# A transformer stack ordered by a planner: a longer modelled delay from ScalarE to TensorE, and five scheduler constants

## Chip, core and metric

The kernel runs on one core of one Trainium2 chip. The metric is the time of one execution on the device in microseconds, as the median over several runs. Five engines work beside each other, each through its own list in order: TensorE (PE in the profile), VectorE (DVE), ScalarE (ACT), GpSimd (POOL) and the DMA queue of SyncE (SP).

## What is computed

Two layers of attention and two of a feed-forward network over 2048 tokens of width 448, with the same weights in both rounds. There are 16 heads of width 28, and the hidden width is 1792.

```python
def _A_ref(x, wqkv, wo):            # S = 2048, D = 448, H = 16, Dh = 28
    qkv = (x @ wqkv).reshape(B, S, 3, H, Dh).transpose(2, 0, 3, 1, 4)
    q, k, v = qkv[0], qkv[1], qkv[2]
    p = softmax(einsum("bhqd,bhkd->bhqk", q, k) * Dh ** -0.5)
    o = einsum("bhqk,bhkd->bhqd", p, v)
    return o.transpose(0, 2, 1, 3).reshape(B, S, D) @ wo
def _B_ref(x, w1, b1, w2, b2):
    h = relu(einsum("bsd,df->bsf", x, w1) + b1)
    return einsum("bsf,fd->bsd", h * h, w2) + b2

x = x + _A_ref(layernorm(x), A_wqkv, A_wo)
x = x + _B_ref(layernorm(x), B_w1, B_b1, B_w2, B_b2)
x = x + _A_ref(layernorm(x), A_wqkv, A_wo)
x = x + _B_ref(layernorm(x), B_w1, B_b1, B_w2, B_b2)
```

## The kernel before

**Units and groups.** Queries are cut into blocks of 256 (the last two of layer 1 into blocks of 128), heads into four sets g of four. A pass is one block, one g and a range of keys. A unit is 512 columns of scores of one head: two tiles of 128 keys by 256 queries, or four by 128. There are 2048 units, 1024 for each layer. `s_stream` puts three units at a time into a tile `sc` of three PSUM banks, of which there are two, so TensorE can be two groups ahead of ScalarE at most. `e_stream` takes the exponential of a group on ScalarE (L835), into one of 11 buffers `pt` (NPT). `p_stream` multiplies with V (L984, "PV"), up to two blocks of keys at a time, accumulating into `oT`.

**The takeover.** `apart` may give the third unit of a group to VectorE, which computes the exponential by a polynomial: `a_unit` and `a_rest`, five instructions (L891, L905, L911, L917, L924). ScalarE's instruction on that group is then 1024 columns wide, not 1536. The unit taken is the next in order, or, when fewer than LAG units remain of the pass, one of the next pass. VectorE has two working sets for this (`R_v`; `v_i`/`v_e`, and a stretch of the K tile not in use). `apart` declines when no set is free, when the load of VectorE over the last 14 us of the plan is above BUSY (0.95), or, where `behind` is true, above LOW (0.8). `behind` compares the chain work done with a straight line given by LINES: from unit a to unit b, n chains. A chain's work is counted as 0.8 for each addition after the output projection, 1 for each full activation tile, 2.8 for each addition after the second matrix, and in layer 0 another 6 for the next layer's Q, K and V; so 14.2 (1.6 + 7 + 5.6) or 20.2 in all for a block.

**The chains.** When all heads of a block are ready, `chain` runs the output projection, layer norm, the first matrix with relu and square, the second matrix, and in layer 0 the Q, K and V of layer 1. VectorE empties most of its PSUM tiles (L1162, L1115, L576, L604 and others). Such work goes to TensorE between the score groups.

**The planner.** The whole order of instructions is decided before launch by a list scheduler, `Planner`. Streams offer their next operation; `earliest` works out when it could start from the modelled ends of what it depends on, plus the delay LAT of the producing engine, and when buffers come free. Those same delays are added when a buffer is released. `run` takes the candidate with the earliest start, priorities deciding ties. Work for TensorE other than scores ("filler") is admitted only if it ends before the score group's due time plus `slack()`:

```python
due = next((c[3][2].ready for c in cands if c[1] == 0), None)
ok = [c for c in cands if c[2] != "PE" or c[1] == 0 or c[0] + c[3][2].dur <= due + self.slack()]
```

`slack()` is SLACK less 512/1200 for each unit that is missing in the group before. The planner's durations are n/1200 + 0.05 us for an exponential over n columns, 0.22 for a group of scores, 0.04 + 0.22 for each block of keys of PV, and 0.1 for changing the shape in which the array is used. Scores are followed by the exponential after 0.25 us.

**Repeats and heating.** Where TensorE's load would be low, scores are issued again, up to three times more (`o.more`, and `again` at L801: as many repeats of 0.22 us as fit before the end of the exponential before, less 0.30 us). `heat` (L1205) also issues idle matmuls (L1220).

**PV and its waits.** `p_stream` prefers key blocks that are ready. It waits for the next exponential rather than for an unfinished unit of VectorE, as long as the oldest group concerned is less than NPT - KEEP groups behind ScalarE (L963).

Of the kernel before, what the change touches and what calls it, by code (L numbers as in the profile page):

```python
# [35 lines left out]
DCLK = 0.2  # L36
OWN = 2
HALF = 320
LINES = ((280, 1312, 7.6), (1440, 2040, 6.6))
MARGIN = 2.0  # L40
LOW = 0.8
TURNS = 1
# [7 lines left out]
GATE = [None, None, ('Q', 0, 0, 0), ('Q', 0, 0, 0), ('s', 8), ('s', 8), ('s', 8), ('s', 8)]  # L50
EARLY = 2
AHEAD = (range(0, 4), range(0, 4), range(0, 4))
SLACK = 0.5
WINDOW = 2.8
C_PRIO = 1.5
V_PRIO = 7.0
# [7 lines left out]
V_WAIT = 5.5  # L64
NEAR = 9
FAR = 15
KEEP = 3
LAG = 5
LEAD = 20
LAST = 690  # L70
BUSY = 0.95
# [46 lines left out]
        self.need, self.got, self.more = need, [], 0.0  # L118


LAT = {"PE": 0.25, "ACT": 0.22, "DVE": 0.10, "POOL": 0.15, "DMA": 2.0, "-": 0.0}


class Planner:
# [3 lines left out]
    def __init__(self):  # L128
# [5 lines left out]
        self.turns = lambda: False  # L134
        self.slack = lambda: SLACK

# [9 lines left out]
    def earliest(self, o):  # L146
        t = 0.0
        for d in o.deps:
            if not isinstance(d, Op):
                d = self.tok.get(d)  # L150
            if d is None or d.end is None:
                return None, None
            same = d.eng[0] == o.eng[0] and len(o.eng) == 1
            t = max(t, d.end + d.lat + ((0.03 if same else 0.10) if d.eng[0] == "DVE" else
                                (0.0 if same and d.eng[0] != "DMA" else LAT[d.eng[0]])))
        acq = o.acq() if callable(o.acq) else o.acq
# [15 lines left out]
    def run(self):  # L172
        while self.streams:
# [9 lines left out]
            if due is None:  # L183
                due = next((c[0] + c[3][2].dur + LAT["ACT"] for c in cands if c[1] == 1), None)
            if due is not None:
# [20 lines left out]
            for a in o.rel:  # L206
                a.got.append(o.end + o.lat + LAT[e])
                if len(a.got) == a.need:
# [9 lines left out]
def kernel(  # L218
# [214 lines left out]
    def slack():  # L433

        n = gbuf[-2]["n"] if len(gbuf) > 1 else 3
        return SLACK - (3 - n) * 512 / 1200

# [251 lines left out]
    def behind(i):  # L689

        l = 0 if i < LINES[0][1] else 1
        a, b, n = LINES[l]
        return done[l] < (min(i, b) - a) / (b - a) * n * per[l] - MARGIN
# [10 lines left out]
    def apart(i, now, us, soon=SOON):  # L704
# [6 lines left out]
        j = i  # L711
        if i + LAG > ends_at[units[i][0]]:
            j = ends_at[units[i][0]] + 1
# [9 lines left out]
        if held[0] + 1 > min(sum(r.n for r in pd_free(units[k])) for k in (i, j)):  # L723
            return None
        if any(pl.tok.get(d) is None or pl.tok[d].end + LAT["DVE"] > now for d in needs(units[j])):
            return None
# [13 lines left out]
    def needs(unit):  # L740
        pi, kb, r, hh = unit
        l, qb, g, *_ = passes[pi]
        t0, nt = blocks[l][qb]
        return [("K", l, g, kb + i) for i in range(r)] + [("Q", l, g, t0 + i) for i in range(nt)]

    def s_stream():
        while at[0] < len(units):
# [5 lines left out]
            def fn(e, gi=gi, us=us, js=js):  # L753
# [45 lines left out]
                if short > 0 and gi > 0:  # L799
                    last = ("e" in gbuf[gi - 1] and gbuf[gi - 1]["e"].end) or pl.clock["ACT"] + 1.35  # L800
                    again = max(0, min(MORE, int(min(o.room, last - LAT["PE"] - 0.05 - o.end) / 0.22)))  # L801
                o.more = 0.22 * again
# [131 lines left out]
    def p_stream():  # L934


        for pi, (l, qb, g, kbs, first, last) in enumerate(passes):
# [18 lines left out]
            while todo:  # L956
                now = [kb for kb in todo if done(kb)][:some]
                if len(now) < min(some, len(todo)):
                    kb = next(kb for kb in todo if not done(kb))
                    if ("u", pi, kb) not in pl.tok or any(k < 3 and ("e", gi) not in pl.tok for gi, k, _ in where[pi, kb]):  # L960
                        yield from got(kb)
                        continue
                    if (e_now[1] - min(gi for gi, _, _ in where[pi, kb]) < NPT - KEEP and e_now[1] < len(gbuf) - 1  # L963
                            and len(todo) > len(now) + 1):
# [306 lines left out]
```

## Time and profile before

| | |
|---|---|
| median of 5 runs | 882.87 us (882.46 to 883.41) |
| the profiled execution | 882.87 us, span 881.0 us |
| ScalarE busy | 866.9 us (98%), 707 instructions |
| TensorE busy | 825.7 us (94%), 12796 matmuls |
| VectorE busy | 794.7 us (90%), 1568 instructions |
| GpSimd busy | 39.3 us (4%) |
| exponentials on ScalarE | 683: 528 of 1536 columns, 155 of 1024 |
| units on VectorE | 154 (87 in the first working set, 67 in the second) |
| granted TensorE clock | 1.000 of full speed |

The span is the time from the first to the last instruction of one profiled execution; 1.87 us of its time lie outside. Busy time is the union of an engine's records. A row "A <- B: us, times, longest" of the waits says how long A's engine sat idle until B released it. Records of ScalarE overlap, so its busy time hides short gaps; the starts of neighbouring records do not.

### The profile page before, as it was taken

The page shows a single profiled execution, that of the slowest core. Times are in us where ns is not written, and L with a number is a line of the kernel's source. Part 1 is how long each engine was busy: PE and PEld are TensorE (multiplying, and loading weights), DVE is VectorE, ACT ScalarE, POOL GpSimd, SP SyncE. Part 2 cuts the span into 40 slices and gives each one's busy share as a digit, 9 for nine tenths or more (in the row PEclk, how much of TensorE's full clock was granted, in tenths as well). Part 3 has the DMA queues.
Part 4 walks back from the last instruction along what each step waited for, and adds up shares of the span by engine and source line. Part 5 has one row for each costly group of instructions (what it writes and reads, how often), then busy time and mean ns, then how long its engine had stood idle before and what let it go on. Part 6 is the DMA issues. An engine that isn't in the chain of part 4 may idle for free.

```text
span 881.0 us, 29066 instructions
## 1 busy us (share of the span) xinstructions
PE 825.7 (94%) x12796; PEld 452.9 (51%) x12796; DVE 794.7 (90%) x1568; ACT 866.9 (98%) x707; POOL 39.3 (4%) x98
## 2 busy tenths in 40 slices
PE   8999999999999999999999999899999999998998
PEld 4555554545545445455554545444545454545566
DVE  7988999999999899999989999999989999999854
ACT  8999999999999999999999999999999999999995
POOL 3100000001010000100001000000000000000000
PEclk9999999999999999999999999999999999999999
DMA  9100100000000000000000000110000000000100
GB/s 253 52 3 3 27 15 15 14 15 16 14 3 14 14 15 15 10 7 15 1 2 2 1 2 3 27 28 27 23 10 20 25 20 20 19 8 15 32 20 13
DMA packets 33914, 18.43 MB, mean 21 GB/s; under 512 B 18874, under 2 KB 33339, under 8 KB 33788
## 3 DMA queue, kind: packets, MB, share of 16 engines
q1 hardware_dynamic: 33788, 16.58, 6.8%
q8 instruction: 100, 1.64, 0.7%
q14 instruction: 26, 0.21, 0.1%
HBM read 14.26 MB, written 2.07 MB: 19 GB/s over the span
## 4 chain that ended last, share of the span: by engine, by line
ACT 74%; issue 11%; PE 10%; DVE 4%; SPq 0%; DMA 0%; POOL 0%
ACT pt L835 74%; PE mt L554 4%; PE sc L810 3%; PE oT L984 2%; PE sc L554 1%; SPq L304 0%; DMA x_sb<-in_A_x_dram 0%; DVE st L449 0%; DVE v_i L917 0%; DVE K_sb L891 0%; DVE v_i L891 0%; DVE v_e L911 0%; PE mt L1220 0%; DVE K_sb L911 0%; PE tp L494 0%
## 5 line engine op out<-in xcount | busy, mean ns | idle before, releaser
L835 ACT ACTIVATE pt<-sc 128x1536 bf16<-128x1536 f32 (+1 forms) x683 | 851.9, 1546 | 1.5 <-PE sc L810 1.4
L810 PE MATMUL sc<-Q_sb,K_sb 32*128 32x256 bf16 (+1 forms) x5818 | 321.7, 265 | 45.2 <-ACT pt L835 39.8
L810 PEld LDWEIGHTS <-K_sb 32*128 32x128 bf16 x5818 | 152.3, 92 | 223.0 <-issue 192.2
L984 PE MATMUL oT<-pt,V_sb 128*32 128x256 bf16 (+1 forms) x4034 | 151.9, 268 | 0.4 <-DVE xnT L506 0.3
L554 PE MATMUL mt<-xnT,w 128*128 128x256 bf16 (+1 forms) x912 | 119.8, 270 | 1.8 <-DVE xnT L506 0.6
L984 PEld LDWEIGHTS <-V_sb 128*32 128x32 bf16 x4352 | 91.6, 96 | 46.1 <-issue 43.1
L554 PEld LDWEIGHTS <-w 128*128 128x128 bf16 x952 | 78.6, 98 | 36.8 <-issue 28.9
L1162 DVE TENSOR_SCALAR r<-mt 128x512 bf16<-128x512 f32 x106 | 72.5, 684 | 8.3 <-PE mt L554 7.4
L554 PE MATMUL mt<-w,V_sb 128*128 128x448 bf16 (+2 forms) x288 | 67.9, 346 | 0.0
L891 DVE TENSOR_SCALAR v_i<-sc 128x512 int32<-128x512 f32 x87 | 59.6, 685 | 9.2 <-PE sc L810 8.7
L917 DVE SCALAR_TENSOR_TENSOR v_i<-v_i 128x512 f32<-128x512 uint16 x87 | 59.5, 684 | 1.3
L911 DVE SCALAR_TENSOR_TENSOR v_e<-v_i,v_e 128x512 f32<-128x512 uint16 x87 | 59.5, 684 | 0.8
L891 DVE TENSOR_SCALAR K_sb<-sc 128x512 int32<-128x512 f32 x67 | 45.8, 684 | 7.8 <-PE sc L810 7.5
L917 DVE SCALAR_TENSOR_TENSOR K_sb<-K_sb 128x512 f32<-128x512 uint16 x67 | 46.1, 688 | 1.4
L471 POOL TENSOR_TENSOR ve<-mv,eps_t 128x2 f32<-128x2 f32 (+1 forms) x34 | 9.5, 279 | 827.7 <-DVE mv L450 827.7
L911 DVE SCALAR_TENSOR_TENSOR K_sb<-K_sb 128x512 f32<-128x512 uint16 x67 | 45.9, 685 | 0.4
L1220 PE MATMUL mt<-xn,ident 128*128 128x448 bf16 x127 | 44.1, 356 | 1.3 <-DVE oT_sb L1007 0.4
L1115 DVE TENSOR_TENSOR x_sb<-x_sb,mt 128x448 bf16<-128x448 bf16 (+2 forms) x63 | 37.9, 601 | 7.5 <-PE mt L554 7.3
L449 DVE BATCH_NORM_STATS2 st<-x_sb 128x6 f32<-128x448 bf16 x64 | 39.7, 620 | 1.7 <-DMA x_sb<-in_A_x_dram 1.2
L554 PEld LDWEIGHTS <-V_sb 128*128 128x128 bf16 x302 | 24.9, 98 | 24.6 <-issue 10.1
L905 DVE TENSOR_SCALAR v_e<-v_i 128x512 int32<-128x512 int16 x87 | 36.5, 420 | 0.4
L984 PE MATMUL oT<-V_sb,V_sb 128*32 128x256 bf16 (+1 forms) x182 | 32.4, 274 | 0.0
(104 smaller groups left out, 792.9 us busy)
## 6 DMA issues: line engine op xcount, KB each, us to landing
rec<-scr SPq DMA_DIRECT2D x56, 128.0 KB
x_sb<-in_A_x_dram SPq DMA_DIRECT2D x8, 224.0 KB
out_dram<-x_sb SPq DMA_DIRECT2D x15, 112.0 KB
w<-in_B_w_dram SPq DMA_DIRECT2D x1, 1568.0 KB
w<-in_B_w_dram SPq DMA_DIRECT2D x1, 1344.0 KB
dn<-oT_sb SPq DMA_DIRECT2D x56, 4.0 KB
V_sb<-in_A_wqkv_dram SPq DMA_DIRECT2D x4, 168.0 KB
scr<-dn SPq DMA_DIRECT2D x28, 8.0 KB
```

What stands on the lines that cost most here:

```text
L449: nc.vector.bn_stats(out=st[:, :], in_=x_sb[:, t0 + j, :])
L554: nc.tensor.matmul(box["t"][:, c0:c0 + n], lhsT=lhsT() if callable(lhsT) else lhsT, rhs=rhs, start=a, stop=b)
L810: nc.tensor.matmul(dst[k][:, i * nt * P:(i + 1) * nt * P], lhsT=K_sb[l][rows, g, (kb + i) * P:(kb + i + 1) * P], rhs=Q_sb[rows, g, t0 * P: ...
L835: t = nc.scalar.activation(out=pt[:, 0:n], in_=gbuf[gi]["sc"][:, 0:n], func=AF.Exp, scale=float(np.log(2.0)) * 2.0 ** -FRAC)
L891: t = nc.vector.tensor_scalar(out=box["i"], in0=two(src), scalar1=EXP_BIAS, scalar2=EXP_LOW, op0=ALU.add, op1=ALU.max)
L905: nc.vector.tensor_scalar(out=box["e"], in0=box["n"], scalar1=2.0 ** 22, scalar2=EXP_BASE, op0=ALU.mult, op1=ALU.add)
L911: nc.vector.scalar_tensor_tensor(out=flt("e"), in0=box["f"], scalar=root, in1=flt("e"), op0=ALU.add, op1=ALU.mult)
L917: nc.vector.scalar_tensor_tensor(out=flt("i"), in0=box["f"], scalar=lin, in1=box["f"], op0=ALU.add, op1=ALU.mult)
L984: nc.tensor.matmul(box["t"][DHP * hh:DHP * hh + DHP, 0:n], lhsT=V_sb[l][:, kb + i, 4 * g + hh, :], rhs=p[:, c0:c0 + n], start=begin and kb ...
L1115: nc.vector.tensor_tensor(out=x_sb[:, tb, lo:hi], in0=x_sb[:, tb, lo:hi], in1=t[:, 0:hi - lo], op=ALU.add)
L1162: nc.vector.tensor_scalar(out=r[:, 0:w], in0=t[:, 0:w], scalar1=0.0, scalar2=None, op0=ALU.max)
L1220: nc.tensor.matmul(t[:, 0:D], lhsT=ident[:, :], rhs=xns[0][:, 0:D], start=True, stop=True)
```

## The change

Six constants change: the modelled delay LAT from ScalarE, and five of the scheduler's. No operation is added or removed in the code; what differs is the order that the planner writes out, which units go to VectorE, and how many repeats there are.

```diff
-LINES = ((280, 1312, 7.6), (1440, 2040, 6.6))
+LINES = ((280, 1312, 7.4), (1440, 2040, 7.0))
...
-SLACK = 0.5
+SLACK = 0.42
...
-KEEP = 3
-LAG = 5
+KEEP = 5
+LAG = 8
...
-LAT = {"PE": 0.25, "ACT": 0.22, "DVE": 0.10, "POOL": 0.15, "DMA": 2.0, "-": 0.0}
+LAT = {"PE": 0.25, "ACT": 0.32, "DVE": 0.10, "POOL": 0.15, "DMA": 2.0, "-": 0.0}
```

LAT enters `earliest` (when an operation that depends on ScalarE can start) and the release of the `sc` tiles. SLACK enters `slack()`. KEEP enters L963, LAG L712, and LINES `behind`.

## Prediction

> **What bounds the kernel now.** I read the page's table of engines first, then the groups by line and form, then the waits.
>
> ```profile
> PE 825.7 (94%) x12796; PEld 452.9 (51%) x12796; DVE 794.7 (90%) x1568; ACT 866.9 (98%) x707; POOL 39.3 (4%) x98
> ACT 74%; issue 11%; PE 10%; DVE 4%; SPq 0%; DMA 0%; POOL 0%
> ```
> ```profile
> L835 ACT ACTIVATE pt<-sc 128x1536 bf16<-128x1536 f32 x528 | 744.7, 1640 | 1.5 <-PE sc L810 1.4
> L835 ACT ACTIVATE pt<-sc 128x1024 bf16<-128x1024 f32 x155 | 178.1, 1225 | 0.0
> ```
> ```profile
> PE sc L810 <- ACT pt L835: 39.8, 110, 0.7
> ACT pt L835 <- PE sc L810: 1.4, 3, 0.7
> ```
>
> ScalarE is the bound: 98% busy, 74% of the chain, and by the waits only 1.4 us late for scores. The last figure misleads. A record of 1640 ns cannot be the cost of an exponential, since 528 such would be 866 us alone. Taken start to start, two neighbours stand 1.330 us apart after a wide (1536) one and 0.903 us after a narrow (1024) one, at the undisturbed pace; the records overlap. What lies above that pace is hidden idleness. The chain of waits around 486 us shows one place:
>
> ```profile
> 485.87 1.45 ACT pt L835
> 487.32 0.04 issue
> 487.37 1.26 ACT pt L835
> ```
>
> 485.87 to 487.37 is 1.50 us where 1.33 would do: 0.17 us lost, though nothing is listed as idle. TensorE's rows there, in the timeline:
>
> ```profile
> 485.70 0.61 PE L554 MATMUL mt<-xnT,w 128*128 128x256 bf16 x4
> 486.14 0.35 PE L1220 MATMUL mt<-xn,ident 128*128 128x448 bf16 x1
> 486.43 0.83 PE L810 MATMUL sc<-Q_sb,K_sb 32*128 32x256 bf16 x18
> ```
>
> Score matmuls, x18 instead of x6, so issued three times over, start at 486.43 and release the exponential 0.94 us later. Over all neighbours in the trace the steps exceed the pace by 9.7 us: 0.85 us at the opening, 6.6 us in 88 places of over 20 ns, and 2.2 us in grains under that. I split the 6.6 us by the time from the first score matmul to the exponential: 46 places have the shortest, 0.50 us (scores simply began late: 3.5 us); 27 have 0.94 (two repeats: 1.5 us); 15 lie between (1.6 us).
>
> The span adds up: 9.6 us before the first exponential; 528 x 1.330 + 155 x 0.903 = 842.2; 2.7 for other ScalarE work among the early ones; 9.7 excess; 16.8 from the last exponential's end (863.3 + 0.9) to 881.0. This execution took 882.87 us, 1.87 outside the span, and it is the median of the five runs, so differences carry over unchanged.
>
> Two things can therefore move the time: the excess, and how many score units VectorE takes over. The groups stay at 683 = 2048/3, since a unit taken away leaves a narrow group. Each takeover saves 1.330 - 0.903 = 0.427 us.
>
> **What the Trainium skill says.** Perfetto Trace Analysis, "DVE / Act Engine Instruction", says that a record runs until the write is acknowledged, and that the semaphore's propagation follows unrecorded. The trace agrees: records exceed their step by 0.31 us (1640 - 1330) and 0.32 (1225 - 903), and in 41 places where TensorE had clearly been idle the score matmul starts 0.05 us after the record's end. The true delay from the end of the step is thus about 0.36 us; the planner believes 0.22 and will believe 0.32. TensorE: Matmul & The Clock Gate, "The mechanism", says matmuls are strict FIFO, so filler already issued cannot be overtaken; 486.14 above agrees.
>
> **The change, part by part.**
>
> *LAT and SLACK.* No instruction is added; the list order is drawn again. Filler before due scores may end until due + SLACK: 0.22 + 0.50 = 0.72 us after the step before, 0.32 + 0.42 = 0.74 after; with 0.1 for the switch of mode, scores start at 0.82 or 0.84. Behind a wide group the trace has room until 1.33 - 0.50 = 0.83. Behind a narrow one the limit falls by 0.427: 0.39 becomes 0.41, against 0.903 - 0.50 = 0.40. So the permitted lateness hardly moves (0.02 us worse), and SLACK has spent what LAT would give there. What improves is the planner's clock after a score group that waited for ScalarE: believed 0.14 us too early, then 0.04. All filler behind it inherits that error, as do the repeats at L801, whose limit (0.37 us after the step for two) is compared with an earlier start than the real one. If all 88 places gained 0.1 us, their sum would fall by 5.5 us. Scores that waited for filler inherit no error; I take half for the two-repeat and the late places and a third for the rest: 0.7 + 1.4 + 0.4 = 2.5 us. The redrawn list is also the order of the queues of SP and GpSimd: the copies of the softmax denominators (dn, scr, rec) and the two rstd instructions of a layer norm move with their steps. VectorE waits 2.5 us for rec and 7.8 us for rstd in the whole run, ScalarE never, so I count nothing there; uncovered, it would be a part of the second rival. The bounds: 5.5 gained, or 1 lost (the extra 0.02 us at half of the steps that are near the limit, plus redrawn order).
>
> *SLACK, as a cost.* From the end of scores to the next due point plus SLACK there is 1.33 - 0.22 + 0.50 = 1.61 us before, 1.53 after. PV (0.48) and two first-layer chunks (0.443 each) with two switches (0.2) need 1.566: they fit before and not after. A chunk of 0.44 us moves to the next gap. TensorE can carry it: of 5818 score matmuls 4352 are needed (the PV weight loads, 4352, count the same), so 1466 repeats and 127 heating matmuls (L1220) can give way. VectorE's evictions come up to 1.3 us later; that is covered while it has other work, and it costs nothing as long as the count holds. If the cover is gone, see the second rival.
>
> *LINES.* "behind" lowers VectorE's permitted load from 0.95 to 0.80. At unit 1980 (834 us) the trace has 98 activations and 58 additions of L1115; with layer 0's 56 and 32 off, that is 42 + 6 x 7.2 + 1.6 = 86.8 of work. The old line asks 540/600 x 6.6 x 14.2 - 2 = 82.3, the new one 87.5. It bites by under one chunk near the end: at most two takeovers lost, +0.9 us, with chain work earlier in return. For layer 0 the line falls and is slacker: zero. I take 0.2 us.
>
> *KEEP and LAG.* PV waits outright for VectorE's oldest unit from 6 groups behind rather than 8; no exponential waits for a pt buffer in the trace, so the older margin hid nothing that I can price. LAG sends takeovers in the last 8 (not 5) of 32 units of a pass to the next one: 3/32 of 154, about 14 units, are others than before. This helps the end of a pass and keeps results longer. Neither is visible in the trace; bounds are 4 takeovers either way, 1.7 us, and I take zero, as gains and losses have one mechanism.
>
> *Tail.* From 864.2 us it is a latency chain whose listed waits stay; +/- 0.5 us.
>
> *Sum:* -2.5 + 0.2 = -2.3, rounded to 880.5 us; with the count's +/- 1.7 it lies between 878.5 and 882.5.
>
> **The rivals.** A measurement of this kernel can tell about 0.2%, 1.8 us, from no change.
>
> First: the error of the planner's clock isn't what makes scores late, and the new order has as many late places as the old. For it: both errors leave the permitted 0.82 to 0.84 at the hardware's 0.83. Against: the 0.94 us places rest on the belief directly. Time 882.7.
>
> Second, slower: the shorter window starves VectorE, and takeovers are lost. One costs VectorE 0.685 + 0.420 + 0.684 + 0.686 + 0.683 = 3.16 us. Between 100 and 800 us it works 654 of 700 us, and most of what idleness it has is waiting for TensorE:
>
> ```profile
> DVE v_i L891 <- PE sc L810: 8.7, 10, 2.1
> DVE oT_sb L1007 <- PE oT L984: 8.5, 10, 2.4
> ...
> DVE r L1162 <- PE mt L554: 7.4, 18, 1.5
> DVE x_sb L1115 <- PE mt L554: 7.3, 5, 2.6
> ```
>
> If deferred chunks add a wait of 1.3 us in some 20 places, 26 us or 8 takeovers are lost: +3.4 us, and about 886 with 0.5 of the stalls unrepaired and late chains at the tail. It decides from 10 lost takeovers if the stalls fall as forecast, from 4 if they don't. Against it: there are 104 us of displaceable filler.
>
> Third: the 46 us of idle VectorE time are used better, as ends of passes wait less. With 5 more takeovers (-2.1) and the stalls: 878.0.
>
> That the change doesn't do what it says is part of the first: 0.32 is still short of 0.36.
>
> **How the numbers follow.** Forecast 0.40 (of it 0.30 faster beyond 0.2%, 0.10 within); first rival 0.16, within; second 0.31 (0.30 slower, 0.01 within); third 0.13, faster. So faster 0.43, within 0.27, slower 0.30. The forecast's own range is 878.5 to 882.5; taking in most of both outer cases gives 876.5 to 887.0.
>
> **What would show it.** Right: 683 exponentials again; 150 to 158 narrow; excess over the pace at 6 to 8 us instead of 9.7; fewer places with 0.94 us from scores to exponential; the last exponential starting near 861. Wrong: under 148 narrow groups, with longer waits of VectorE for L554 and L810 (second); excess still over 9 us (first); or a tail over 17.5 us after the last exponential.

## The result, and the profile after

The changed kernel takes 884.40 us (median of 26 runs; 883.74 to 885.49), the kernel before 882.56 us beside it (46 runs). The ratio is 1.002, with a 95% interval of 1.0015 to 1.0025: slower by 0.2%, where I had forecast 880.5 us. The profiled execution took 883.88 us, 1.01 more than before's; its span is 882.1 us. So the pair of traces shows 1.1 us of the 1.8 us between the medians: before's is 0.3 us slower than its median, the changed kernel's 0.5 us faster, the second fastest of 26. Where the rest lies, no trace here tells.

The engines and the chain of the changed kernel, from its page:

```profile
PE 822.9 (93%) x12455; PEld 444.2 (50%) x12455; DVE 788.1 (89%) x1558; ACT 868.0 (98%) x707; POOL 38.5 (4%) x98
ACT 73%; issue 12%; PE 10%; DVE 4%; SPq 0%; DMA 0%; POOL 0%; ACTq 0%
```

The exponentials of the changed kernel by form (count, then busy us and mean ns of one):

```profile
L835 ACT ACTIVATE pt<-sc 128x1536 bf16<-128x1536 f32 x530 | 750.3, 1661 | 1.9 <-PE sc L810 1.7
L835 ACT ACTIVATE pt<-sc 128x1024 bf16<-128x1024 f32 x153 | 179.7, 1256 | 0.0
```

Its waits between ScalarE and TensorE, and VectorE's longest for TensorE (us in total, times, longest):

```profile
PE sc L810 <- ACT pt L835: 40.2, 122, 0.9
ACT pt L835 <- PE sc L810: 1.7, 4, 0.9
...
DVE v_i L891 <- PE sc L810: 10.7, 14, 2.3
DVE r L1162 <- PE mt L554: 10.0, 18, 1.6
DVE x_sb L1115 <- PE mt L554: 9.6, 10, 2.6
```

ScalarE is still the bound. There are two narrow groups fewer (153 for 155), so two units went from VectorE back to ScalarE, and VectorE is busy 6.6 us less, with longer waits for scores (L891 on v_i, 8.7 to 10.7), first-layer chunks (L1162, 7.4 to 10.0) and second-layer sums (L1115, 7.3 to 9.6). TensorE issues 374 score matmuls fewer (5444 for 5818): fewer repeats.

**A reading of ScalarE that I lacked.** My prediction took the distance between the starts of two exponentials as their cost and counted what exceeded 1.330 us as lost. Here are the two records around its example, the exponentials that start at 485.87 and 487.37 us in the kernel before (groups of ScalarE's operations, each of a window that holds a single one; the number just before the second bar is its duration in ns):

```profile
L835 ACT ACTIVATE pt<-sc 128x1536 bf16<-128x1536 f32 x1 | 1.7, 1707 | 0.0
```
```profile
L835 ACT ACTIVATE pt<-sc 128x1536 bf16<-128x1536 f32 x1 | 1.6, 1554 | 0.0
```

They end at 485.868 + 1.707 = 487.575 and 487.365 + 1.554 = 488.919: 1.344 us apart. The second started 0.167 us late and its record is 0.153 us shorter. It is so everywhere. In all fourteen kernels measured here the median distance between the *ends* is 1343 ns for a wide exponential and 917 for a narrow one. Between the 5th and the 95th percentile lie 1342 to 1344 and 916 to 918 in the kernel before. Undisturbed starts are 13 to 14 ns closer together than ends, so they run ahead, and each record reaches that much further beyond its step than the one before. ("Step" is the 1.330 or 0.903 us between starts.) Right after a true wait a record reaches 0.12 us beyond its step; in before's trace half of all records reach 0.27 to 0.37 us, the longest 0.58. Scores that come late first use that lead up, and only beyond it does ScalarE lose time: in the fourteen traces 175 exponentials end more than 0.03 us late, and every one of their records is back at 0.120 to 0.127 us beyond the step. So the starts show idleness where there is none; the ends do not.

Counted by ends, the span is the end of the first exponential, the other exponentials at 1.343 and 0.917 us, true lateness, and the tail after the last one ("opening" is what the part before 21 us has beyond this pace, for other work and for late scores):

| us | first end | opening | paced (narrow groups) | lateness after 21 us | tail | span |
|---|---|---|---|---|---|---|
| before | 11.09 | 2.42 | 849.90 (155) | 1.40 | 16.20 | 881.0 |
| changed | 10.89 | 2.82 | 850.75 (153) | 1.68 | 15.96 | 882.1 |
| difference | -0.20 | +0.40 | +0.85 | +0.28 | -0.24 | +1.1 |

Of before's 1.40 us of lateness 1.08 belong to one exponential, which ends at 21.3 us. What the planner could have won from late scores in the remaining 840 us was about 0.3 us, not 6.6.

### The profile page after: what moved, and what is told of

Same layout as the page of the kernel before. It is cut to its first block, busy times and chain, and to the rows that moved or that the text cites. A ratio compares the mean times of both kernels' runs of the same rounds, so it can differ in the third digit from the quotient of the medians.

```text
span 882.1 us, 28379 instructions
## 1 busy us (share of the span) xinstructions
PE 822.9 (93%) x12455; PEld 444.2 (50%) x12455; DVE 788.1 (89%) x1558; ACT 868.0 (98%) x707; POOL 38.5 (4%) x98
## 4 chain that ended last, share of the span: by engine, by line
ACT 73%; issue 12%; PE 10%; DVE 4%; SPq 0%; DMA 0%; POOL 0%; ACTq 0%
ACT pt L835 73%; PE sc L810 3%; PE mt L554 3%; PE oT L984 2%; PE sc L554 1%; DVE st L449 1%; PE mt L1220 0%; PE tp L494 0%; SPq L304 0%; DMA x_sb<-in_A_x_dram 0%; DVE v_i L891 0%; DVE x_sb L1115 0%; DVE v_i L917 0%; DVE v_e L911 0%; DVE xn L521 0%
## 5 line engine op out<-in xcount | busy, mean ns | idle before, releaser
L810 PE MATMUL sc<-Q_sb,K_sb 32*128 32x256 bf16 (+1 forms) x5444 | 309.3, 265 | 45.7 <-ACT pt L835 40.2
L810 PEld LDWEIGHTS <-K_sb 32*128 32x128 bf16 x5444 | 142.6, 92 | 224.9 <-issue 189.0
L554 PE MATMUL mt<-xnT,w 128*128 128x256 bf16 (+1 forms) x880 | 118.4, 272 | 1.8 <-DVE r L1162 0.5
L554 PEld LDWEIGHTS <-w 128*128 128x128 bf16 x952 | 78.6, 97 | 38.2 <-issue 29.8
L1162 DVE TENSOR_SCALAR r<-mt 128x512 bf16<-128x512 f32 x106 | 72.3, 682 | 10.6 <-PE mt L554 10.0
L891 DVE TENSOR_SCALAR v_i<-sc 128x512 int32<-128x512 f32 x85 | 58.2, 684 | 11.1 <-PE sc L810 10.7
L554 PE MATMUL mt<-w,V_sb 128*128 128x448 bf16 x274 | 68.0, 355 | 0.0
L1220 PE MATMUL mt<-xn,ident 128*128 128x448 bf16 x160 | 54.9, 357 | 1.8 <-DVE oT_sb L1007 0.6
L891 DVE TENSOR_SCALAR K_sb<-sc 128x512 int32<-128x512 f32 x67 | 45.8, 684 | 8.4 <-PE sc L810 8.0
L1115 DVE TENSOR_TENSOR x_sb<-x_sb,mt 128x448 bf16<-128x448 bf16 x63 | 38.5, 611 | 9.7 <-PE mt L554 9.6
L554 PEld LDWEIGHTS <-V_sb 128*128 128x128 bf16 x302 | 24.9, 98 | 24.4 <-issue 10.3
L924 DVE SCALAR_TENSOR_TENSOR V_sb<-v_i,v_e 128x512 bf16<-128x512 f32 x49 | 33.4, 681 | 0.2
```

The lines of the kernel that those rows point to most:

```text
L554: nc.tensor.matmul(box["t"][:, c0:c0 + n], lhsT=lhsT() if callable(lhsT) else lhsT, rhs=rhs, start=a, stop=b)
L810: nc.tensor.matmul(dst[k][:, i * nt * P:(i + 1) * nt * P], lhsT=K_sb[l][rows, g, (kb + i) * P:(kb + i + 1) * P], rhs=Q_sb[rows, g, t0 * P: ...
L891: t = nc.vector.tensor_scalar(out=box["i"], in0=two(src), scalar1=EXP_BIAS, scalar2=EXP_LOW, op0=ALU.add, op1=ALU.max)
L1115: nc.vector.tensor_tensor(out=x_sb[:, tb, lo:hi], in0=x_sb[:, tb, lo:hi], in1=t[:, 0:hi - lo], op=ALU.add)
L1162: nc.vector.tensor_scalar(out=r[:, 0:w], in0=t[:, 0:w], scalar1=0.0, scalar2=None, op0=ALU.max)
L1220: nc.tensor.matmul(t[:, 0:D], lhsT=ident[:, :], rhs=xns[0][:, 0:D], start=True, stop=True)
```

## The experiments

Theory A says that the list as drawn decides: takeovers, gaps and tail. Its numbers are the end of the list by the planner's clock, plus some 8 us for the span and 1.87 us more for the time. Theory B is my prediction's: the excess of the starts is lost time, and a truer delay wins some of it back. Theory C, formed on reading the ends, says that ScalarE is paced by its ends and that excess of the starts costs nothing. "The planner's clock" is the time that the planner itself notes for an operation of its list.

The rows of all runs, counted as above:

| us | ratio of times (95%) | first end + opening | paced (narrow) | lateness | tail | span |
|---|---|---|---|---|---|---|
| e1 delay alone | 1.0106 (1.0091 to 1.0122) | 13.96 | 851.17 (152) | 4.27 | 19.46 | 888.9 |
| e2 LAG alone | 1.0022 (1.0014 to 1.0031) | 13.25 | 851.17 (152) | 1.87 | 16.37 | 882.7 |
| e3 LINES alone | 1.0047 (1.0034 to 1.006) | 13.79 | 849.90 (155) | 1.46 | 20.80 | 885.9 |
| e4 changed, LAG 5 | 1.0145 (1.0131 to 1.0159) | 14.46 | 850.75 (153) | 5.07 | 24.06 | 894.3 |
| e5 one repeat less | 1.0043 (1.0027 to 1.0058) | 14.11 | 849.90 (155) | 6.72 | 16.18 | 886.9 |
| e6 nor heating | 1.0096 (1.0081 to 1.011) | 13.74 | 849.90 (155) | 12.75 | 16.15 | 892.5 |
| e7 true duration | 1.0148 (1.0135 to 1.0161) | 13.39 | 849.04 (157) | 15.22 | 16.41 | 894.1 |
| e8 constants alone | 1.0079 (1.0066 to 1.0092) | 13.67 | 850.75 (153) | 6.81 | 16.15 | 887.4 |
| e9 delay and SLACK | 1.0075 (1.0061 to 1.0089) | 14.70 | 849.90 (155) | 6.18 | 16.49 | 887.3 |
| e10 list with 157 | 1.0004 (0.9996 to 1.0012) | 13.48 | 849.04 (157) | 2.42 | 16.04 | 881.0 |
| e11 another with 157 | 1.0003 (0.9995 to 1.0011) | 13.31 | 849.04 (157) | 2.55 | 16.36 | 881.3 |
| e12 list with 161 | 1.0009 (1.0001 to 1.0017) | 13.44 | 847.34 (161) | 4.63 | 16.22 | 881.6 |

The delay alone:

```diff
-LAT = {"PE": 0.25, "ACT": 0.22, ...
+LAT = {"PE": 0.25, "ACT": 0.32, ...
```

> The kernel before with the delay from ScalarE alone raised to 0.32; SLACK, KEEP, LAG and LINES stay. Theory A (the list decides): what counts is how the list is drawn, and the planner's own clock shows it. For before that clock ends the last exponential at 855.8 us and everything at 872.8, for the changed kernel at 857.4 and 874.2; the chip needs some 8 us more for both. For this list it says 860.8 and 880.6, so a span near 888.7, about 0.8% slower than before, with 152 narrow groups and excess over the pace that is not smaller than before's 8.8 us after the first 20 us. Theory B (the clock's truth decides, as in my prediction): the excess falls by 2 us or more with the delay alone, and the constants are what cost time; 879 to 881 us.

Measured 891.71 us with 152 narrow groups. The traced execution, the fastest of four, has a span of 888.9, theory A's number; the median is 1.1% slower, not 0.8%. The longer delay alone costs 1.27 us in takeovers, 2.9 us in lateness, 3.3 us in the tail. Of the lateness 1.0 us follows a stretch of low clock (0.57 from 837 to 841 us). The excess of the starts after the first 20 us, which by theory B should have fallen by 2 us from 8.8, is 12.0.

LAG alone:

```diff
-LAG = 5
+LAG = 8
```

> The kernel before with LAG 8 in place of 5 alone. Theory A: three takeovers fewer (152 narrow groups for 155), +1.3 us of pace; the planner's clock ends at 873.8, 0.9 us later than before, so about 883.7, 0.1% slower. Theory B: if LAG is what cost the time in the changed kernel, all of its 1.8 us appear here, 884.4 or more.

Measured 884.69, ratio 1.0022. The three takeovers are gone, as A said: 1.27 of the trace's 1.7 us. The time is higher than A's 883.7 and as high as B's 884.4, so the time alone does not tell A from B here; the split by ends, with no other term above 0.5 us, speaks for A.

LINES alone:

```diff
-LINES = ((280, 1312, 7.6), (1440, 2040, 6.6))
+LINES = ((280, 1312, 7.4), (1440, 2040, 7.0))
```

> The kernel before with the new LINES alone. The planner's list is the same up to unit 1982 or so, where the steeper line turns one takeover down for a moment. Theory A: same pace, same excess, last exponential at the same time; by the planner's clock the tail is 3.2 us longer (876.0 for 872.8), so 885.8, 0.35% slower. Theory B, as I priced it in the prediction: 0 to +0.9 us through takeovers, tail no longer: 882.6 to 883.5.

Measured 886.59. Pace and lateness are before's; the tail is 20.8 us instead of 16.2. ScalarE after the last exponential in this kernel (start and duration, and in brackets how long it was idle before, and for what):

```profile
863.76 1.38 ACT L835 ACTIVATE pt<-sc 128x1024 bf16<-128x1024 f32 x1
870.28 0.60 ACT L1160 ACTIVATE r<-mt 128x512 bf16<-128x512 f32 x1 [5.14 <-PE mt L554]
```

and before the change:

```profile
865.70 0.60 ACT L1160 ACTIVATE r<-mt 128x512 bf16<-128x512 f32 x1 [0.90 <-DVE oT_sb L1007]
```

The first activation of the last two blocks comes 4.6 us later. The two lists part only at unit 1951 (not 1982), where one takeover is turned down and the last chains are reordered; the number of narrow groups is the same. This trace is of the slowest of five executions, 1.4 us above the median, and its clock is 0.57 from 869 to 873 us, within the tail; so not all of the 4.6 us need be the list's, of which the plan has 3.2. I had allowed 0.9 us for LINES, and none of it in the tail.

The changed kernel with LAG back at 5:

```diff
-LAG = 8
+LAG = 5
```

> The changed kernel with LAG back at 5. Theory A: by the planner's clock the last exponential ends at 860.6 and everything at 882.7, 8.5 us later than with LAG 8, because of 3.7 us in which the plan itself leaves ScalarE idle and a tail 5 us longer: 892 to 893 us, 1% slower than before. So the new LAG does not cost time in the changed kernel, it gives back what the delay took. Theory B (constants cost time): faster than the changed kernel, 881 to 883.

Measured 895.55, span 894.3. So LAG 8, which costs 0.2% in the old list, is worth 1.2% in the new one: 8.1 us of tail and 3.4 of lateness. Of the tail the plan has 5 us; the clock was 0.57 from 874 to 882 us, so the rest isn't clearly the list's. The lateness has one main place, where layer 1 first needs keys of the later blocks; below it is called the bridge to layer 1. In the timeline of this kernel:

```profile
545.91 1.05 PE L554 MATMUL mt<-xnT,wk 128*128 128x256 bf16 x8
546.99 0.69 DVE L576 CAST K_sb<-mt 128x512 bf16<-128x512 f32 x1 [1.66 <-PE mt L554]
547.74 0.61 PE L810 MATMUL sc<-Q_sb,K_sb 32*128 32x256 bf16 x12 [0.79 <-DVE K_sb L576]
548.25 1.94 ACT L835 ACTIVATE pt<-sc 128x1024 bf16<-128x1024 f32 x2 [2.72 <-PE sc L810]
```

K of layer 1 is projected at 545.9, written at 547.7, multiplied, and only then does ScalarE go on, after 2.7 us. The chain of layer 0 arrived too late for the next layer. The same place shows in e8 (3.7 us at 550 us by ends), e9 (3.8 at 549) and e7 (9.4 at 554); in before and the changed kernel nothing is lost there. These gaps are drawn by the planner: its own list leaves ScalarE idle there for 3.3 us in this kernel, 3.3 in e8, 4.2 in e9 and 7.6 in e7.

Then theory C. The repeats first:

```diff
-                for i in list(range(4)) * (again + 1):
+                for i in list(range(4)) * (again if again > 1 else again + 1):
```

> The kernel before, same list, same takeovers; where the planner asks for two or three repeats of a score group, one fewer is issued (the time is still set aside in the plan). Theory B (my prediction: what starts show above a pace of 1.330 us is lost): the class of 27 places with 0.94 us from scores to exponential disappears, 1.5 us less, 881.0 to 881.3. Theory C, which the ends of the records suggest: ScalarE's ends are 1.343 us apart behind wide and 0.917 behind narrow groups, whatever the starts do; starts run ahead and are pulled back, so the excess of the starts isn't idleness, and at most 0.3 us can be had. The starts' excess keeps its sum, in other places; the time stays at 882.6 within 0.5.

Measured 886.59: slower, which neither theory said. Two things are mixed in it, and the stretches part them (us busy and instructions by engine, then the granted clock):

```profile
core 0: us, PE busy (x) PEld busy (x) DVE busy (x) ACT busy (x) POOL busy (x), PEclk, DMA share, GB/s
430.00:480.00 50.00, 47.07 (x662) 24.44 (x662) 45.57 (x84) 50.00 (x42) 1.30 (x2) 1.00 0.01 2
480.00:530.00 50.00, 46.76 (x690) 24.50 (x688) 47.09 (x90) 50.00 (x42) 1.06 (x4) 1.00 0.01 2
...
700.00:715.00 15.00, 14.82 (x173) 6.96 (x167) 11.87 (x24) 12.44 (x11) 0.17 (x1) 0.67 0.01 2
```

From 700 to 715 us the clock is 0.67 in the mean, and 3.0 us of lateness by ends lie between 705 and 711 us. Two shorter stretches, from 351 to 355 and from 744 to 748 us, have 0.57; of the 5.3 us of lateness that this kernel has over before, 4.7 lie in these three or within 5 us behind them. Before has 1.00 in all three, so the repeats hold the clock up there. The seven executions agree: 883.40 us with a mean clock of 1.000, 888.68 with 0.990. The stretch from group 300 to group 500 (390 to 638 us) ran at 1.00. In it before has 13 of the places with 0.94 us from scores to exponential, which my prediction priced at 0.66 us; here none is left. From end to end the 200 exponentials took 248.187 us before and 248.185 here. This is the plainest test of the reading: the class that I meant to win back was removed, and nothing came of it.

The same without the heating matmuls, `heat()` issuing none:

> As the run before, and the heating matmuls of heat() in the main part aren't issued either. Theory B: the late places behind L1220 go too, 3.5 to 4 us less than before in all, 878.8 to 879.4. Theory C: no change but for the granted clock, 882.6 within 0.5; if the clock falls below 1.00 because TensorE is less busy, slower.

Measured 891.37. The mean clock of the run is now low:

```profile
core 0: 892.5 us, clock 0.967
```

The time thus tells of the clock and not of the starts. But the trace has a long stretch at 1.00, from the end of exponential 305 to that of 430 (400 to 555 us). These 125 took 155.542 us, the same as before's and e5's, though the 15 heating matmuls that before has there are gone. So the heating matmuls did not cost time there either, as C says.

Then the planner's duration of an exponential:

```diff
-... Op("ACT", n / 1200 + 0.05, fn, ...
+... Op("ACT", n / 1200 + 0.0633, fn, ...
```

> The kernel before with the planner's duration of an exponential at n/1200 + 0.0633 us instead of 0.05. That draws another list (157 narrow groups), which by the planner's clock ends at 888.2, the last exponential at 871.2. Theory C: the drift of 8.7 us between the planner's clock and the chip over the exponentials was this 0.0133 us times 683 = 9.1 us; with it repaired the last exponential ends within 1 us of the planner's clock and the span is 887 to 888.5, 0.7% slower (a worse list). Theory B: the drift is stalls; the chip ends 8 us after the planner again, 896.

Measured 895.78, near B's number, and C's was wrong. The last exponential ends at 877.7 us, 6.4 beyond the planner's clock. By ends, though, this is no drift: from group 20 to group 100 chip and planner now keep the same distance to 0.01 us, where before they part by 1.06 us (80 x 0.0133). What comes on top is 15.2 us of lateness in 20 places, and the largest by far is the bridge to layer 1:

```profile
553.55 1.94 ACT L835 ACTIVATE pt<-sc 128x1024 bf16<-128x1024 f32 x2 [9.29 <-PE sc L810]
```

Of its 9.4 us the plan itself had 7.6; of the 15.2 us another 7.6 were in no plan. So the drift was the duration, as C says, but a consequence had escaped me. My explanation is that a ScalarE which the planner believes to be faster than it is leaves the other engines waiting for it, and that this is a margin in which late scores cost nothing; made exact, the plan has no such margin. That is not shown. The clock is a rival: the granted clock was 0.66 from 209 to 214 us and 0.57 from 547 to 555, at the bridge, and about 3.6 of the 7.6 us lie there. e12 below has the exact duration too and, at a clock of 1.000, loses 3.2 us more than before; so something besides the clock is at work, but whether it is the margin or the other list was not separated.

The constants without the delay:

```diff
-LAT = {"PE": 0.25, "ACT": 0.32, ...
+LAT = {"PE": 0.25, "ACT": 0.22, ...
```

> The changed kernel with the delay from ScalarE back at 0.22: the constants alone. Theory A (the list decides): by the planner's clock 876.5, so a span near 884.5 and a time near 886.3, 0.4% slower than before; then both halves of the change are slower than both together, and neither has an effect of its own to be added up. Theory B: without the truer delay the constants' loss stands alone: 2 us or more slower than the changed kernel, 886.4 or more, with a larger excess of the starts.

Measured 889.74, 3.4 us above A's number; B's "2 us or more slower than the changed kernel" holds, and the excess of the starts is larger, as B said. But 3.7 of its 6.81 us of lateness lie in the one gap at the bridge, of which the plan itself has 3.3; that is a gap of the list, not late filler. Together with e1 it makes a square: old delay and constants 882.6, new delay alone 891.7, new constants alone 889.7, both 884.4. The effects do not add.

The pair of my argument, delay 0.32 and SLACK 0.42 on the kernel before:

> The kernel before with delay 0.32 and SLACK 0.42, without the other three constants: the pair of which my prediction said that it keeps the permitted lateness and makes the clock truer. Takeovers stay at 154, so nothing of the pace hides what the pair does. Theory A: by the planner's clock 878.0 (4.9 us in which the plan leaves ScalarE idle), span 886, time 888, 0.6% slower. My prediction's reasoning gives 2.5 us less than before, 880.

Measured 889.06. With takeovers unchanged, the pair costs 0.75%, all of it lateness (6.18 for 1.40 us) and the opening. A forecast 888, my prediction 880.

Last, lists with more takeovers, chosen by the planner's clock. The first two change constants only:

> The kernel before with SLACK 0.49, LAG 4, BUSY 0.97, HOLD1 6, NLP 3.5, chosen by the planner's clock alone: 156 takeovers (157 narrow groups), plan end 871.3, the last exponential at 854.7. Theory A and C: two takeovers more, -0.85 us, and a shorter plan, so the span is 879.4 and the time 881.2, 0.15% faster than before. Theory B has no ground for a change but the takeovers: 881.8.

> A second list with 157 narrow groups: the kernel before with SLACK 0.45, LAG 6, NEAR 8, BUSY 0.97, HOLD1 6, SOON 0.5, NLP 3.5; plan end 872.0, last exponential 854.6. Theory A and C: span 880.2, time 882.0, 0.1% faster. If the chip needs more than 10 us beyond the plan here, the planner's clock can't be trusted for differences below 1 us.

Measured 883.07 and 882.86: no difference from before. The 0.86 us of pace are there, and lateness rose by 1.0 and 1.2 us. The chip needs 9.7 and 9.3 us beyond the plan's end, not 8, so differences of 1 us in the planner's clock don't carry over.

> The planner's duration of an exponential at n/1200 + 0.0633, with SLACK 0.51, WINDOW 2.4, V_LATE 3.4, NEAR 8, LAG 6, BUSY 0.98, SPAN 12, HEAT 0.70, NLP 3.5: 160 takeovers (161 narrow groups), plan end 879.2, last exponential 862.3. Five takeovers more than before are worth 6 x 0.427 = 2.6 us of ScalarE's pace. If the plan were kept, the span would be 879.5 and the time 881. After the run with the true duration, where the chip lost 6.4 us to late scores beyond the plan, I expect the spare time that the too short duration gave to be missed here too: 3 to 6 us of real lateness, 884 to 887, slower than before in spite of the pace.

Measured 883.41, ratio 1.0009; my 884 to 887 was too dark. It has six takeovers more, not the five of the text above. The forms of this kernel:

```profile
L835 ACT ACTIVATE pt<-sc 128x1536 bf16<-128x1536 f32 x522 | 732.4, 1590 | 1.9 <-PE sc L810 1.6
L835 ACT ACTIVATE pt<-sc 128x1024 bf16<-128x1024 f32 x161 | 178.2, 1163 | 0.6 <-PE sc L810 0.2
```

Six narrow groups more are worth 2.56 us of pace, as counted, and 3.23 us more of lateness take them back, in 23 places. The mean records are 50 to 62 ns shorter than before's: ScalarE's lead is smaller, scores are more often just in time. No list tried beats both kernels; e10 and e11 equal before.

In the eight runs for which theory A named a time (e1 to e4 and e8 to e11) the kernel was slower than A's number each time, by 0.8 to about 3.5 us. A had the direction right in six of them, but not in e10 and e11, which it put below before.

## Why the prediction was wrong, step by step

**What bounds the kernel:** right as to the engine, wrong as to its pace. The step that failed is "Taken start to start, two neighbours stand 1.330 us apart ... what lies above that pace is hidden idleness". The 9.7 us of excess were for the greater part the pace itself: 528 x 0.013 + 155 x 0.014 = 9.0 us. The price of a takeover, 0.427, barely moves by ends (1.343 - 0.917 = 0.426). The gain of 2.5 us was to come from an excess of which 0.3 us could be had; in the pair of traces the terms are +0.85 us of pace for two lost takeovers, +0.68 of lateness and opening, -0.20 at the first exponential and -0.24 in the tail: +1.1.

**LAT and SLACK:** forecast -2.5 us, bounds -5.5 and +1. The direct forecast on the class with two repeats came true in the starts, by luck: it fell from 27 places and 1.54 us to 20 and 0.77, a gain of 0.77 where I had said 0.7. But the new list has only 69 groups with two repeats for 98, so the share that is late stayed at 28 to 29%; there were fewer repeats, not better placed ones. And it was worth nothing, as e5 shows.

That 0.32 is the truer delay isn't shown either. The 0.31 us by which records exceed their step is the lead for the most part, and no fixed delay: in 126 places of before's trace where TensorE had been idle for over 0.1 us until an exponential ended, the score matmul starts 0.05 us after the record's end, but 0.18 to 0.59 us after the end of the step. From the pace of the ends, in which the lead drops out, I estimate the delay as 1.450 - 1.343 + 0.05 = 0.16 us, below both settings. The limits of 0.83 and 0.40 us, beyond which scores were to cost time, are those of a ScalarE without a lead; the lead moves them by some 0.2 us, and by up to 0.46 us at the longest record. Lateness and opening together rose by 0.68 us, inside the bound of 1. That the pair alone costs 0.75% (e9) lies outside both bounds: I had priced the permitted lateness and not the redrawn list, above all the bridge to layer 1, which no row of before shows because it was just met.

**SLACK, as a cost:** VectorE does wait longer for L554 and L810, as the second rival said. It lost 2 takeovers, not 8. Which constant lost them can't be told apart: LAG alone loses 3, the delay alone 3, delay and SLACK none.

**LINES:** allowed 0.9 us through takeovers. Alone it costs 3.8 us by the median, mostly through the order of the last chains (e3), and in the changed kernel the tail is 0.24 us shorter than before's. The term was mis-sized and misplaced.

**KEEP and LAG:** taken at zero with 4 takeovers either way. LAG alone is 3, inside the bound; in the new list it is worth 11 us, through tail and bridge, which I had not priced (and in part, perhaps, through the clock). KEEP was not run apart.

**Tail:** forecast +/- 0.5 us, measured -0.24. Right.

**Rivals:** the first, with as many late places as before, comes nearest: 98 places of excess after for 89 before, counting the opening. But its 882.7 missed the two takeovers and the opening. The second had the right sign and the right waits, at a quarter of its size. The third did not come; its parts, -2.1 and -2.5, give 878.3, not 878.0. The stated test "excess still over 9 us (first)" fired: 10.7 us in all. "Last exponential starting near 861" was 864.9.

## What to carry to other kernels

Take the pace of a saturated engine from the ends of its records and look for its losses there: starts may run ahead, and a late start behind a long record costs nothing. In a kernel whose order a scheduler draws, a constant has no effect of its own, only a list, and the list decides by its cliffs, here the bridge between layers and the last chains; a model made truer can draw a worse one, as e7's exact duration did, so each candidate is measured. That a modelled duration that is too short serves as a margin is a guess of mine; that its repair needs measuring like any other change is what e7 shows.

## What the hardware showed that I had not expected

ScalarE's exponentials end 1343 ns (1536 columns) and 917 ns (1024) apart, 63 to 64 ns over the 1280 and 853 ns of n/1200, while undisturbed starts are 1330 and 903 apart. A record of 1536 columns thus grows by 13 ns with each neighbour in an unbroken row, from 1.45 us after a true wait to 1.6 or 1.7 us and 1.89 at most, and its length tells how much lateness it can still take: about the part beyond 1.45. TensorE's granted clock depended on the repeats: with 612 of 5818 score matmuls left out it fell to 0.67 in the mean from 700 to 715 us, to 0.57 in two stretches of 4 us, and was 1.00 from 390 to 640 us; without 127 heating matmuls as well its mean over the span was 0.967. A fall was itself followed by late scores in e1, e5, e6 and e7.
